# A new table of order, engines and buffer slots for a hand-scheduled attention and maxout kernel

## The chip, the cores and the metric

The kernel runs on one core of one Trainium2 chip. The metric is the time of one execution on the device in microseconds (us). The kernel before took 281.86 us, the median of three runs (281.57 to 282.61).

## What is computed

There are two stages. The first is linear attention with a feature map over exponentials; the second is a feed-forward layer that takes the largest of three products. The sizes are 8 batches, 8 heads, 576 positions, head size 64, 128 features; then 4,608 tokens of 512, a hidden size of 768.

```python
def phi(x):
    proj = np.einsum('bhsd,df->bhsf', x, w_phi)
    proj = proj - np.max(np.abs(proj), axis=-1, keepdims=True)
    return np.concatenate([np.exp(proj), np.exp(-proj)], axis=-1)
q_p, k_p = (phi(q), phi(k))
kv = np.einsum('bhsf,bhsd->bhfd', k_p, v)
z = np.sum(k_p, axis=2)
num = np.einsum('bhsf,bhfd->bhsd', q_p, kv)
den = np.einsum('bhsf,bhf->bhs', q_p, z)[..., None] + 1e-06
x = num / den                      # to [4608, 512]
h = np.maximum(np.maximum(x @ w1, x @ w2), x @ w3)
out = h @ w_out
```

## The kernel before

**Units and chunks.** The attention is cut into 16 units, each of four heads of one batch. Units 2b and 2b+1 together give the 512 features of batch b. The feed-forward layer is cut into nine chunks: chunk b takes the first 512 positions of batch b, and chunk 8 takes the last 64 positions of all batches.

**What one unit does.** POOL's queue loads q and k as bf16 (Lq, line 383, and Lk, line 393), SP's queue the last 64 positions of q (Lt, line 426) and v (Lv, line 435). For the first four units PE transposes q and k (T, line 459); for the others SP issues transposing DMAs (T, line 478). PE multiplies with the feature matrix (G, line 496, and M, lines 593 and 600). DVE takes the largest absolute values (rk and rq, line 500), ACT the exponentials of k (ek, line 504) and q (eq, line 584). POOL scales v by the exponentials of the maxima (va, line 548). PE multiplies keys by values (K, line 567) and queries by the result (N, line 632). DVE combines the two halves (xu, line 641; xw, line 644, which needs xu) and takes the reciprocal (xr, line 689). POOL divides (x, line 690). The result x is transposed into place by PE for the first two units (X, line 707), by SP's DMA for the others (X, line 722).

**What one chunk does.** PE multiplies x by differences of the weights (up and up2, line 748); ACT or DVE takes the positive part (t1), DVE the maximum (h). Then PE adds two products in one bank (straight, line 781; down, line 786), ACT or DVE copies the bank to a buffer `osb` (line 796), and SP's or ACT's queue stores it (line 800). There are four `osb` buffers: a copy may overwrite one only when its last store has landed.

**Row modes.** G, M (but its last one) and K use 64 of PE's 128 rows; all other matmuls use 128.

**What sets the order.** Nothing is scheduled by the framework. Every step is a node with its allowed engines, its dependences and its buffers. 1,565 nodes are listed in the order in which the program is made. The string `PLAN` (from line 88) has one word for each node, such as `753S2@135.0`: node 753, on SP (T is PE, D DVE, A ACT, G POOL, S SP), its buffers in the slots 2, and a start time by the planner's account. The words' order is the order of issue: each engine and each DMA queue runs its own nodes in that order, one behind the other. The start times are used once: `fill` puts idle matmuls on a tile of ones (line 911) into PE's gaps up to 30 us, so that PE is kept busy.

```python
for word in PLAN.split():
    what, start = word.split("@")
    at = next(i for i, c in enumerate(what) if c.isalpha())
    n, slots = nodes[int(what[:at])], iter(what[at + 1:])
    n.eng, n.start = ENGINES[what[at]], float(start)
    n.end = n.start + n.costs[n.eng] + 0.2
    for b in n.bufs:
        if b.index is None:
            b.index = int(next(slots), 36)
    order.append(n)
```

Nodes that the text names: 103 loads k of unit 1; 753 and 1031 load v of units 10 and 14; 749 loads q of unit 10 and 755 transposes it; 1267 and 1299 are stores, 1310 and 1302 copies into `osb`; 767 is an exponential of unit 10; 609 is the transposing DMA of x of unit 7; 666 is an N of unit 8; 1060 and 956 are steps of POOL for units 14 (va) and 12 (x); 1117 is a G of unit 15; 27, 106 and 110 are transposes by PE of units 0 and 1; 1553 is a down of chunk 8.

Of the kernel before, what the change touches and what calls it, by code (L numbers as in the profile page):

```python
# [88 lines left out]
9G0@1.2 10S0@0.8 3A@1.1 1D@0.8 2G@1.9 16S0@1.3 0G@2.1 103G1@2.7 104G@7.2 4A@1.8 12D@4.0 8G@7.5 6D@4.2 11A@4.0  # L89
19T0@4.5 5A@4.3 7A@4.6 20D0@5.2 25T1@5.8 187S1@2.9 13S@4.5 26D@6.4 29T23@6.3 102G@8.2 30A0@6.7 51T45@6.9 73T67@7.1 110T0@8.0  # L90
105S1@5.1 34A0@7.2 106T1@8.1 18S2@5.7 53D0@7.3 33A@7.7 32D0@7.9 35D@8.5 107D1@9.1 119T53@9.9 75A0@8.2 31A@8.7 260G2@8.9 77A@9.1
74A0@9.6 186G3@9.6 259G@10.4 111D@9.7 76A@10.1 112T21@10.1 188G@11.1 124A1@10.6 123A1@11.1 126T06@10.3 52D@9.9 128A@11.5 17G@11.3 122D1@10.5
115D@11.1 127A@11.8 1166G@11.5 15D@11.7 27T4@12.1 14D@12.0 117A@12.1 120A@12.5 121A@13.0 1167G@12.3 1169G@13.0 130D1@12.2 28D@12.5 43T76@12.8
21T4@13.0 261G@13.8 129D@12.7 46D@13.1 47D@13.5 54A0@13.6 113A@13.8 78T0@13.3 22D@13.8 36T56@14.3 118D@14.1 125D@14.7 56G0@14.0 44A@14.3
114A@14.5 79A@15.0 23T4@14.6 39D@15.3 40A@15.3 24D@15.9 42D@16.3 48T23@16.4 55G@15.1 137A1@15.8 139G1@16.2 80A@16.0 45A@16.2 50D@16.9
116A@16.5 185G@17.3 58A@17.0 108T4@16.7 37A@17.2 334S0@11.6 140G@18.0 263T0@17.2 57A@17.7 59G@18.2 60G@19.3 267T7@17.7 68T13@17.9 61G@20.4
38A@17.8 49D@17.5 81A0@18.3 109D@18.1 264D2@18.7 268D@19.3 41A@18.5 72A@18.9 71A@19.4 138G@20.5 141A@19.9 131T25@18.8 142G@21.6 144A@20.1
62T46@19.1 64A0@20.2 69A@20.3 63A@20.8 70A@21.0 134T07@19.7 132D@19.5 190T3@20.1 65T26@20.6 1168G@22.7 133D@20.1 156T54@21.2 135D@20.7 82T01@21.6
67A@21.4 66A@21.6 161T6@21.9 136D@21.3 158A1@21.7 191D3@21.8 85T27@22.1 159A1@22.2 143G@23.4 83D0@22.4 160A@22.7 86D@22.9 333G0@24.5 157A@23.2
84D@23.3 164A1@23.7 265T3@22.6 163A@23.9 87D@23.7 332G@25.2 162A@24.1 145T04@23.4 146A1@24.4 151T21@23.9 147A@24.5 194T5@24.3 266D@24.1 155A@24.7  # L100
152A@25.2 195D@24.7 1180T7@24.4 93T60@24.8 153A@25.6 88D0@24.9 89G0@26.0 1181D0@25.0 1172G@27.6 90T34@25.1 154A@26.1 94D1@25.6 148T57@25.7 149A@26.6
91D@26.0 283T62@26.3 1178T3@26.5 165T15@27.0 285A0@26.7 284A0@27.0 95D@26.4 92D@26.8 1176T0@27.3 150A@27.3 287D0@27.2 96D1@27.5 1179A@27.4 168T47@27.7
97G@29.7 286D0@27.6 335G@30.9 196T26@28.1 98T3@28.5 166D2@28.0 1177A@28.3 169D@28.4 200A1@29.2 198A1@29.7 176T14@28.9 197A@30.1 167D@28.8 170D@29.2
276T50@29.4 177D0@29.6 99D@30.0 277A@30.6 173T71@30.1 178D@30.4 100T3@31.0 171D2@30.8 202D1@30.9 1170G@31.1 174D@31.5 278A@31.1 281A@31.6 199D@31.9
280A@32.1 175D@32.5 172G1@33.2 1186T4@31.4 1184T7@32.7 192T2@34.0 279D@32.9 210T15@34.6 179D0@33.5 403G1@34.4 337S0@38.0 189S3@39.4 101A@32.5 1187A@33.1
180G@35.1 201A@33.6 203T34@34.7 1185A@34.2 282D@33.6 208A@35.1 1171G@36.3 1173G@38.4 205A@35.6 262S0@40.0 214D1@34.9 269T60@34.9 270A@36.1 274A@36.5
181T7@35.2 1182T5@35.5 1183A@37.0 193D@35.2 183T2@36.8 473S1@40.6 182D@35.8 209D@36.2 204A@37.5 1188T7@37.1 272D@36.8 184D@37.4 213D@37.8 206D@38.1
271A@38.0 1189A@38.6 1194T5@38.4 207A@39.0 301T26@39.3 212A@39.5 275D@38.7 1175G@40.5 294A0@39.8 402G@42.6 1174G@43.3 221A1@40.0 224A0@40.2 305A0@40.3
288T37@39.6 304A0@40.8 303A@41.2 211A@41.7 1195D1@39.4 338S@42.2 336S2@43.9 297A1@42.0 1202T4@39.9 273A@42.1 302A@42.6 404G@45.4 289D@40.0 223G@45.7
612S0@45.8 290D@40.6 1200T5@40.7 1196T3@41.6 222G@47.7 1203D@41.2 291T76@42.6 228T41@42.8 229A1@43.2 1201D@41.8 1197D@42.7 230A1@43.7 218T50@43.0 293D@43.3  # L110
1206T2@43.3 238T3@44.2 1192T6@44.3 220D@43.9 232A@44.2 219D@44.5 406S1@47.4 1207D@45.1 239A@44.6 240A@44.9 1193A@45.4 215T40@45.3 306T53@45.5 292D@45.7
231A@45.8 216D@46.2 217D@46.8 1214T2@45.8 1204T6@46.7 1215D@47.4 310A@46.3 1205D@48.0 307A@46.8 309A@47.3 475S1@50.0 1198T7@47.5 241A0@47.7 339T14@48.5
345D0@48.9 353T03@48.7 233T26@48.8 308A@47.9 1199A@48.6 357D1@49.5 237A@49.2 356D@49.8 342D@50.2 295G@49.8 296G@51.9 234A@49.7 1212T5@49.1 225T73@50.1
405S3@50.6 235A@50.2 236A@50.7 344A1@51.5 472G2@53.9 1213D@50.8 226D0@51.5 355A@51.9 346T26@51.3 227A@52.2 349D@51.8 352D@52.4 1210T5@51.7 1211D@53.0
340A1@52.5 471G@54.6 1208T7@52.5 343A@52.9 1209D@53.6 474G@55.4 242T34@53.6 542G3@55.6 354A@53.4 243D1@54.2 543G@56.3 341A@53.7 351A@54.1 245T50@53.9
246D@54.6 348A@54.6 244D@55.0 347A@55.1 350A@55.6 247D@55.4 298T71@54.3 300A1@56.1 253T35@55.6 250T42@55.9 364A1@56.3 367A0@56.5 314A1@56.6 299D@55.8
# [826 lines left out]
```

## Time and profile before

| What | before |
|---|---|
| median of the runs (lowest, highest) | 281.86 us (281.57, 282.61) |
| span of the profiled execution, first to last instruction | 280.8 us |
| PE, DVE, ACT, POOL busy, share of the span | 96%, 77%, 71%, 58% |
| granted clock of PE | 1.000 |
| packets of DMA, data moved | 76,214; 44.52 MB |

The profile gives the span of one execution; the runs' times also hold what lies around it. Busy time is the time in which an engine works; idle time is listed with what ended it. PE is the matmul unit, PEld its weight loads, DVE, ACT and POOL the vector, scalar and general units, SP the engine that only issues transfers; a name with q at its end is the engine's sequencer. The DMA share is the sum of the packets' times over that of the core's 16 DMA engines; packets overlap, so it can go over 1.

### The profile page before, as it was taken

To read this page: it belongs to the slowest core of one execution; us is meant where nothing else is said; L and a number is where in the kernel's file an instruction comes from. 1 tells how busy PE (TensorE), PEld (TensorE's weight loads), DVE (VectorE), ACT (ScalarE), POOL (GpSimd) and SP (SyncE) were. 2 spreads that over 40 slices of the span, in tenths; PEclk is the share of its full clock that TensorE was granted. 3 is DMA by queue.
4 is the path that set the end of the run, shared out by engine and by line. 5 is a ranking of instruction groups with operands and counts; after the bars stand their busy time and mean duration, and the time that the engine had idled before them with its cause. 6 is when DMAs were issued, how large, how long until landed. Compare 5 with 4: busy or idle time off the path is not lost. (4 is left out here: it accounts for less than half of the span.)

```text
span 280.8 us, 8401 instructions
## 1 busy us (share of the span) xinstructions
PE 268.3 (96%) x3409; PEld 150.8 (54%) x3447; DVE 217.3 (77%) x442; ACT 199.1 (71%) x489; POOL 161.5 (58%) x161
## 2 busy tenths in 40 slices
PE   8789899999999999999999999999999999999993
PEld 5457654576655555555555456655546544444441
DVE  2799989999999969889997899898876871157320
ACT  4799999999999787698978879989589200310001
POOL 4879999998949703897336848393495341000000
PEclk9999999999999999999999999999999999999999
DMA  7999999997999999999999997717130224110253
GB/s 136 300 202 208 207 173 310 260 164 132 171 186 249 236 196 281 169 171 144 189 263 204 188 276 125 151 55 170 39 86 3 77 47 121 40 75 0 82 144 112
DMA packets 76214, 44.52 MB, mean 159 GB/s; under 512 B 52688, under 2 KB 67344, under 8 KB 76176
## 3 DMA queue, kind: packets, MB, share of 16 engines
q1 hardware_dynamic: 59536, 29.21, 49.8%
q0 software_dynamic: 14912, 11.77, 28.7%
q10 hardware_dynamic: 1728, 3.02, 3.0%
q8 instruction: 27, 0.44, 0.7%
q14 instruction: 11, 0.09, 0.1%
HBM read 34.64 MB, written 9.44 MB: 157 GB/s over the span
## 5 line engine op out<-in xcount | busy, mean ns | idle before, releaser
L748 PE MATMUL ups<-xT,w_bf 128*128 128x512 bf16 x414 | 101.3, 379 | 1.0
L584 ACT ACTIVATE Eq<-psm 128x512 bf16<-128x512 f32 (+1 forms) x160 | 81.7, 587 | 5.4 <-PE psm L593 3.1
L548 POOL TENSOR_TENSOR vab<-v_raw,em 128x1152 bf16<-128x1152 f32 (+1 forms) x36 | 68.2, 1907 | 22.9 <-ACT em L542 15.0
L504 ACT ACTIVATE Ek<-psk 128x512 bf16<-128x512 f32 x128 | 72.1, 633 | 8.2 <-PE psk L496 6.3
L748 PEld LDWEIGHTS <-w_bf 128*128 128x128 bf16 x432 | 39.2, 98 | 43.9 <-issue 2.3
L690 POOL TENSOR_TENSOR x_sb<-y,rden 128x640 bf16<-128x640 f32 x32 | 39.9, 1256 | 39.5 <-DVE rden L689 39.0
L786 PE MATMUL ops<-wout_bf,hT 128*128 128x512 bf16 (+2 forms) x214 | 50.5, 373 | 0.3
L758 DVE TENSOR_TENSOR hT<-hT,ups 128x512 bf16<-128x512 bf16 x54 | 35.5, 677 | 13.3 <-PE ups L748 11.1
L500 DVE TENSOR_REDUCE mq<-psq 128x4 f32<-128x512 f32 x64 | 41.2, 682 | 3.5 <-PE psq L496 3.2
L500 DVE TENSOR_REDUCE mk<-psk 128x4 f32<-128x512 f32 x64 | 41.9, 679 | 2.1 <-PE psk L496 1.7
L762 ACT ACTIVATE hT<-ups 128x512 bf16<-128x512 f32 x36 | 21.9, 620 | 24.5 <-PE ups L748 24.4
L641 DVE TENSOR_TENSOR y<-psn,sq 128x325 f32<-128x325 f32 x64 | 30.4, 491 | 6.7 <-PE psn L632 4.3
L796 ACT COPY osb<-ops 128x512 f32<-128x512 f32 x20 | 12.2, 608 | 32.3 <-PE ops L786 31.8
L786 PEld LDWEIGHTS <-hT 128*128 128x128 bf16 x222 | 20.6, 98 | 22.5 <-issue 0.2
L632 PEld LDWEIGHTS <-Eq 128*128 128x128 bf16 x640 | 26.3, 98 | 10.3 <-issue 0.4
L644 DVE TENSOR_TENSOR y<-y,psn 128x325 f32<-128x325 f32 x64 | 29.7, 487 | 1.6
L632 PE MATMUL psn<-kv_sb,Eq 128*128 128x65 bf16 x640 | 28.8, 194 | 0.2
L496 PEld LDWEIGHTS <-qkT 64*128 64x128 bf16 x576 | 18.0, 94 | 13.4 <-issue 8.3
L781 PE MATMUL ops<-xT 128*128 128x512 bf16 x87 | 23.7, 380 | 0.5
L567 PE MATMUL kvps<-vab,Ek 64*128 64x65 bf16 x1152 | 22.1, 191 | 0.8 <-POOL vab L548 0.6
L567 PEld LDWEIGHTS <-Ek 64*128 64x128 bf16 x1152 | 20.3, 94 | 3.4 <-issue 1.3
L796 DVE COPY osb<-ops 128x512 f32<-128x512 f32 (+2 forms) x17 | 11.1, 657 | 12.5 <-PE ops L786 12.5
(65 smaller groups left out, 263.9 us busy)
## 6 DMA issues: line engine op xcount, KB each, us to landing
v_raw<-in_v_dram SPq DMA_DIRECT2D x15, 576.0 KB, 6.0
out_dram<-osb SPq DMA_DIRECT2D x23, 256.0 KB, 3.3
qk_bf<-in_k_dram POOLq DMA_DIRECT2D x15, 288.0 KB, 6.9
qk_bf<-in_q_dram POOLq DMA_DIRECT2D x15, 256.0 KB, 8.7
w_bf<-in_moe_w_dram POOLq DMA_DIRECT2D x3, 768.0 KB, 13.2
out_dram<-osb ACTq DMA_DIRECT2D x9, 256.0 KB, 3.4
tail_raw<-in_q_dram SPq DMA_DIRECT2D x16, 64.0 KB, 4.8
wout_bf<-in_moe_w_out_dram POOLq DMA_DIRECT2D x1, 768.0 KB, 19.2
```

The costliest lines, as they stand in the source:

```text
L500: return nd(kind, {"DVE": 0.598 if n == 4 else 0.331}, lambda: nc.vector.tensor_reduce(dst(m()), ps()[:, 0:n, :], AXX, ALU.max, apply_abso ...
L504: return nd("ek", {"ACT": 0.478 if n == 4 else 0.264}, lambda: nc.scalar.activation(dst(Ek[g]()), ps()[:, 0:n, :], EXP, scale=1.0 - 2.0 * ...
L548: made.append(chosen(n_, lambda n_, g=g, t0=t0, t1=t1: (nc.vector if n_.eng == "DVE" else nc.gpsimd).tensor_tensor(vab()[:, g, t0:t1, 0:D] ...
L567: nc.tensor.matmul(kvps[ab]()[:, pr, g, :], lhsT=Ek[g]()[r, t, :], rhs=vab()[r, g, t, :], start=(pr == prs[0] and g + j == 0), stop=(pr == ...
L584: return nd("eq", {"ACT": 0.478 if n == 4 else 0.264}, lambda: nc.scalar.activation(Eq[g]()[:, t0:t0 + n, :], ps()[:, 0:n, :], EXP, scale= ...
L632: nc.tensor.matmul(psn[g]()[:, i, :], lhsT=Eq[g]()[:, t, :], rhs=kv()[:, pr, ab, g, :], start=True, stop=True)
L641: n_ = nd("xu", {"DVE": 0.064 + 0.0676 * n_t}, lambda: nc.vector.tensor_tensor(yv(y()), ps(0), sq_of(sq()).unsqueeze(len(shape) - 1).to_br ...
L644: return nd("xw", {"DVE": 0.064 + 0.0674 * n_t}, lambda: nc.vector.tensor_tensor(yv(y()), yv(y()), ps(1), ALU.add), [n_], [psn[1], y], loc ...
L690: divs[pr] = nd("x", {"POOL": 1.2}, lambda pr=pr, y=y, rden=rden: nc.gpsimd.tensor_tensor(x_sb()[:, pr].rearrange("p t a d -> p a t d"), y ...
L748: nc.tensor.matmul(ups()[:, o * n:(o + 1) * n], lhsT=w_bf[i + (not plain)][:, ct, jj * P:(jj + 1) * P], rhs=tokens_of(ct)[:, cols] if halv ...
L758: nc.vector.tensor_tensor(dst, dst, src, ALU.max)
L786: nc.tensor.matmul(ops_()[:, 0:hi - lo], lhsT=hT()[:, j, tt * P:(tt + 1) * P], rhs=wout_bf[:, j, lo:hi], start=plain and j == 0, stop=(j = ...
```

## The change

Only the string `PLAN` is replaced. The nodes, their work, their sizes and the number of buffers stay. The new table was laid out with an account of when the last part of each transfer lands and of a gap at each change of row mode. It holds the same 1,565 nodes in another order, on other engines where there is a choice, and in other slots. The counts by table:

| What | before | after |
|---|---|---|
| changes of row mode in PE's order | 98 | 94 |
| loads of v issued by SP, by ACT | 15, 1 | 11, 5 |
| copies into `osb` by ACT, by DVE | 20, 17 | 27, 10 |
| positive parts (t1) by ACT, by DVE | 36, 18 | 32, 22 |
| copies of K's result (kv) by ACT, by DVE | 26, 10 | 22, 14 |

A cut of the diff: the first lines, and those that hold the nodes named above.

```diff
-9G0@1.2 10S0@0.8 3A@1.1 1D@0.8 2G@1.9 16S0@1.3 0G@2.1 103G1@2.7 104G@7.2 4A@1.8 12D@4.0 8G@7.5 6D@4.2 11A@4.0
...
-625A1@102.3 529D@102.3 819G@94.0 537D@102.7 633A1@102.8 1294T0@103.0 632A@103.0 530D0@103.1 1285D@103.3 628A@103.3 749G@94.7 629A@103.8 1280T4@103.9 538D1@103.9
...
-753S2@135.0 1324T1@136.4 758A@137.8 781A1@138.3 1303A@138.5 736D@136.8 1325D@137.5 757A@139.0 740T34@137.3 741D2@138.1 1326T5@137.6 743T21@138.5 737D@138.5 738D1@139.1
...
-1031A1@155.0 1033S3@150.2 963S@151.5 1366T5@154.4 1030G@155.0 806D1@154.6 851G@155.2 1356T4@155.3 1367D@155.5 868A0@155.6 1357A@156.4 917T13@156.3 909T67@156.5 913D1@156.8
...
+3A@0.7 1D@0.8 4A@1.3 10S0@0.7 9G0@1.2 103G1@1.9 0G@2.6 16S0@1.1 104G@4.9 17G@5.1 11D@3.5 7D@3.7 5D@3.9 8G@5.3 6D@4.1 12A@3.5 19T0@4.0
...
+616S@95.3 1029S1@96.4 574G@100.1 1283A@103.9 633A@104.3 700T35@103.8 526D@103.4 530D0@103.8 1259S@97.6 635D1@104.0 753A0@104.6
...
+594D@115.4 749G@112.6 755S@117.6 595D@115.8 599D2@116.2 662A0@117.0 698A@117.2 646T07@116.1 659T5@117.3 695A@117.7 660A@118.2
...
+768A1@121.2 661A@121.7 1309T@121.3 663T75@122.6 710D@121.6 1267S@118.7 712G1@120.2 1300T2@122.9 769D1@122.2 664D2@123.2 722A0@122.0
+721A0@122.4 1310A3@122.9 767A1@123.4 1030G@122.3 766D@123.5 671T71@123.8 666T36@124.1 667D@124.6 668D@125.0 672D1@125.4 609S@119.1
+1299A@123.9 890S0@120.5 720A@124.5 764A@124.9 1515G@123.5 1514G@124.3 1301T@124.4 824S@121.7 674T36@125.7 765A@125.4 719A@125.9
+728T7@126.0 1302A1@126.7 714G@125.1 1027G@125.3 1032S1@122.8 1322T4@126.1 1323A0@127.2 730A@127.7 675D@126.2 673D@126.7 676D@127.0
...
+1409D@184.4 1395D@185.2 1048T52@185.1 1045A@184.9 1049A@185.4 1050A@185.7 1031A2@185.9 1052D1@185.8 1051D@186.2 993T16@185.2
```

More of the change, by code (lines that the diff above doesn't have):

```diff
@@ L93 @@
[L93 to L104, printed above, removed]
@@ new lines @@
+1084D@211.1 1418D3@211.5 1419S@212.3 1431S@212.7 1088T53@211.4 1146A@211.9 1439A1@212.1 1450T7@211.7 1152T26@212.6 1089D1@212.1
+1085D@212.5 1086D2@212.9 1153D2@213.1 1090D@213.5 1451D@213.9 1154D@214.5 1442T1@212.9 1432T5@213.7 1433A@214.8 1087G2@213.2
+1149T02@214.6 1150D@215.1 1151D@215.5 1436T3@214.9 1091T76@215.8 1440T5@216.1 1452T0@216.9 1443A@215.3 1092D@216.3 1093D@216.7
+1094D1@217.1 1095G@217.4 1096S@218.8 1446T2@217.8 1155D0@217.2 1437A@216.0 1144A@216.5 1157T17@218.7 1158D0@219.2 1159D@219.6
@@ new lines @@
+1487D@236.8 1493D@237.6 1470A3@232.9 1472T5@237.4 1478T1@238.3 1476T4@239.1 1477A@240.2 1479D@239.4 1491D@240.0 1467A@240.7
+1494T0@240.0 1495D@241.1 1522T3@240.9 1484T4@241.7 1473D@241.7 1485D@242.8 1526T1@242.6 1496T7@243.5 1508T0@244.3 1488T5@245.2
+1542T4@246.1 1462A1@241.3 1527A@243.7 1524T2@246.9 1463S@241.9 1523D@243.4 1489D@246.3 1534T1@247.8 1535D@248.8 1458D0@249.4
+1532T3@248.6 1509T@249.5 1510A2@251.0 1511A@251.5 1530T5@250.8 1540T1@251.7 1525D@250.1 1541D@252.7 1536T6@252.5 1531D@253.3
@@ L202 @@
+"""
 ENGINES = {"T": "PE", "D": "DVE", "A": "ACT", "G": "POOL", "S": "SP"}
```

217 lines of the change are left out of this document (121 added, 96 removed).

## The prediction

> **What bounds the kernel now.** I read the page first, then busy time by stretches, then what PE waited for.
>
> ```profile
> span 280.8 us, 8401 instructions
> ...
> PE 268.3 (96%) x3409; PEld 150.8 (54%) x3447; DVE 217.3 (77%) x442; ACT 199.1 (71%) x489; POOL 161.5 (58%) x161
> ```
>
> ```profile
> core 0: us, PE busy (x) PEld busy (x) DVE busy (x) ACT busy (x) POOL busy (x), PEclk, DMA share, GB/s
> 0.00:33.00 33.00, 28.72 (x478) 20.04 (x478) 25.58 (x59) 26.93 (x74) 26.63 (x40) 1.00 1.12 211
> 33.00:75.00 42.00, 40.73 (x605) 23.86 (x614) 39.57 (x83) 41.18 (x104) 40.78 (x34) 1.00 1.06 202
> 75.00:150.00 75.00, 74.31 (x1004) 41.09 (x1018) 67.63 (x140) 64.48 (x155) 45.69 (x43) 1.00 1.22 208
> 150.00:155.00 5.00, 4.31 (x121) 2.92 (x117) 3.60 (x6) 4.00 (x9) 2.84 (x3) 1.00 1.20 179
> 155.00:277.00 122.00, 120.23 (x1212) 62.89 (x1228) 80.90 (x158) 62.51 (x152) 45.52 (x44) 1.00 0.41 99
> 277.00:281.00 4.00, 0.00 (x0) 0.00 (x0) 0.00 (x0) 0.00 (x0) 0.00 (x0) 1.00 0.40 115
> ```
>
> PE is the bound, and the clock is full throughout, so only PE's idle time can be won: 280.8 - 268.3 = 12.5 us. Some 4 of them lie behind its last matmul, 4.3 in the first 33 us. From 33 to 75 us DVE, ACT and POOL are as full as PE (39.57, 41.18, 40.78 of 42): there PE could not run ahead of them anyway. From 75 to 155 us PE alone is full, and the packets' times fill the 16 DMA engines 1.22 times over. After 155 us everything but PE has room.
>
> The longest waits of PE's own work, and the place of the last one:
>
> ```profile
> PE tps L459 <- DMA qk_bf<-in_k_dram: 1.6, 1, 1.6
> ...
> PE pxT L707 <- issue: 0.7, 1, 0.7
> PE kvps L567 <- POOL vab L548: 0.6, 1, 0.6
> ```
>
> ```profile
> 148.49 2.12 POOL L548 TENSOR_TENSOR vab<-v_raw,em 128x1152 bf16<-128x1152 f32 x1 [1.55 <-DMA v_raw<-in_v_dram]
> ...
> 152.89 1.04 PE L567 MATMUL kvps<-vab,Ek 64*128 64x65 bf16 x54 [0.64 <-POOL vab L548]
> ```
>
> POOL stood 1.55 us for a v load, and PE paid 0.64 of it.
>
> How far may the times in the table be used? Only as distances, and only because the trace follows them:
>
> ```profile
> 9.34 0.72 PE L459 MATMUL tps<-ident,qk_bf 128*128 128x128 bf16 x10 [1.60 <-DMA qk_bf<-in_k_dram]
> ...
> 273.26 2.47 PEld L786 LDWEIGHTS <-hT 128*128 128x128 bf16 x12
> ```
>
> These are entries 110 and 106 (written for 8.0 and 8.1) and entry 1553 (written for 268.7): late by 1.3 and by 4.6. So 260.7 us of the table took 263.9 on the chip, 1.2% more. A distance of 5 us in the table is 5 us on the chip, if nothing between waits. The question is whether transfers fit the distances that the new table leaves.
>
> **The change part by part.** Matmuls, copies and transfers are the same in number; their work is costed at nothing. What changes is who waits.
>
> *Start.* The first transpose waits for the first half of k in both tables: no gain. The 1.60 us wait is for k of unit 1 (entry 103), which now goes ahead of the identity and of a memset:
>
> ```profile
> 2.13 0.22 POOL L330 MEMSET wph_low<- 64x128 bf16 x1
> ...
> 2.81 0.73 POOL L393 DMA_DIRECT2D qk_bf<-in_k_dram  x1
> ```
>
> It is issued 0.68 us sooner, so at best 0.7 of the wait goes. All of the table's lead is bound from above by its two ends, 271.3 against 269.3: 2.0 us. But the time passes through the stretch where DVE is as full as PE, and the new order puts more dependent pairs there:
>
> ```profile
> 24.78 0.49 DVE L641 TENSOR_TENSOR y<-psn,sq 128x325 f32<-128x325 f32 x1
> 25.18 0.89 DVE L644 TENSOR_TENSOR y<-y,psn 128x325 f32<-128x325 f32 x2
> ```
>
> Two independent ones take 0.89, the second starting 0.40 after the first; one that needs the other's result waits its whole 0.49, 0.09 more. Counting DVE instructions that directly follow the one they need, up to 80 us, I find 2 in the old table and 22 in the new one: 20 x 0.09 = 1.8 us of DVE. Bounds -2.0 and +1.8; I take +0.5, since 0.7 of gain against 1.8 of loss is +1.1, and DVE is not full in the first 33 us (25.58).
>
> *Row mode.* Both tables leave about 0.1 us at a change between 64-row and 128-row matmuls; the changes go from 98 to 94. What one costs:
>
> ```profile
> 51.86 1.04 PE L748 MATMUL ups<-xT,w_bf 128*128 128x512 bf16 x4
> 52.83 0.24 PE L567 MATMUL kvps<-vab,Ek 64*128 64x65 bf16 x4
> ```
>
> ```profile
> 252.03 7.77 PE ups L748 x36
> ```
>
> At 7.77 / 36 = 0.216 each, four matmuls issued from 51.86 end at 52.72; the other mode starts at 52.83: 0.11. Four fewer: -0.4.
>
> *The v load of unit 10.* It was entry 753 on SP, 8.5 us ahead of its use; now on ACT, 31.4 ahead. The 0.64 us go; late next for K is only POOL's product itself, 2.12 us long, for which the table leaves its full time: -0.6.
>
> *A new tight chain at 112 to 128 us.* POOL issues q of unit 10 (749@112.6). SP's transpose 755@117.6 waits for it; behind it on SP stand store 1267@118.7, the x transpose 609 and a tail load. The store must land before ACT's copy 1310@122.9 may overwrite its buffer; behind that copy on ACT stands 767, whose bank PE's 666@124.1 needs. Next, store 1299@123.9 must land before ACT's copy 1302@126.7. Distances: 5.0 for the load, 4.2 and 2.8 for the stores. The old table leaves never under 6.2 between a store and the reuse of its buffer. Measured: q loads from 30 to 160 us, stores from 80 to 155, v loads of the whole run:
>
> ```profile
> L383 POOL DMA_DIRECT2D qk_bf<-in_q_dram x11: 750/760/811, 44.4 to 158.6; - x11
> ...
> DMA to landing us min/median/max: 4.9/8.3/12.0
> ```
>
> ```profile
> L800 SPq DMA_DIRECT2D out_dram<-osb x10: 343/534/1148, 81.8 to 154.9; - x10
> ...
> L800 ACTq DMA_DIRECT2D out_dram<-osb x3: 338/354/372, 86.5 to 142.6; - x3
> ...
> DMA to landing us min/median/max: 3.3/6.1/8.5
> ```
>
> ```profile
> L435 SPq DMA_DIRECT2D v_raw<-in_v_dram x15: 368/575/1439, 4.6 to 190.1; - x15
> ...
> L435 ACTq DMA_DIRECT2D v_raw<-in_v_dram x1: 458/458/458, 158.8 to 158.8; - x1
> ...
> DMA to landing us min/median/max: 4.4/6.2/9.4
> ```
>
> At the shortest landings only the last store is late, 3.3 - 2.8 = +0.5. At the medians it is 3.3 + 1.9 + 3.3 = +8.5. The medians come partly from loads issued four in a row, and this one goes alone; so I take 6.5 for the load (+1.5), 5.0 for the first store (+0.8) and 3.3 for the second (+0.5): +2.8.
>
> *The v load of unit 14.* Entry 1031, on ACT, 3.6 us ahead of its use 1060 on POOL; late by 0.8 at the shortest landing, by 2.6 at the median. Behind 1060 stands the division 956, which frees a buffer for DVE, which frees a bank for PE's 1117; about 1.4 us of the table's distances lie between. So 0 to +1.2; I take +0.4, as few transfers run there (share 0.41). The Trainium skill ("DMA: Bandwidth & Descriptors", "Anatomy of one DMA") puts a transfer at about 2.0 us plus bytes over 436 GB/s, an estimate of 3.4 us for these 576 KB, and by it this term would be 0. The trace disagrees: none of 16 landed under 4.4.
>
> *SP to ACT.* Five v loads instead of one go by ACT, 0.46 us of ACT's queue each against 0.58 of SP's. The one that did so landed after 9.4, the longest of all:
>
> ```profile
> v_raw<-in_v_dram ACTq DMA_DIRECT2D x1, 576.0 KB, 9.4
> ```
>
> The same page of the Trainium skill ("Issuing engines are not separate DMA queues") says that this saves issue time alone, as the 16 DMA engines are shared; by that rule, too, the landings above stay as they are. I add nothing.
>
> *End.* Both tables end with a copy and a store on ACT; the 4 us stay.
>
> Sum: 0.5 - 0.4 - 0.6 + 2.8 + 0.4 = +2.7, a span of 283.5. The median of the runs, 281.86, lies 1.1 us over the span; with these the forecast is **284.6 us**.
>
> **The rivals.** *The early lead holds and the transfers fit (faster).* The place is the first 33 us: if DVE's dependent pairs fall where it has room, the lead of the table counts, -1.4 (0.7 of the k load, and as much again from the second half of unit 0, whose transposes, entry 27, stand at 10.1 instead of 12.1); with -0.4, -0.6 and only +0.5 at unit 10: -1.9, 280.0 us. It decides when q of unit 10 lands within 5 us and the stores within 3.3. For it: the shortest q landing is 4.9. Against: the DMA share of 1.22 just there.
>
> *The transfers fit, but no early lead (same).* 0.5 - 0.4 - 0.6 + 0.5 + 0 = 0: 281.9 us. By the Trainium skill's figure above it would come out so.
>
> *Everything lands at the medians (much slower).* 0.5 - 0.4 - 0.6 + 8.5 + 1.2 = +9.2: 291.1 us. For it: in the new table the 30 us from 105 hold eight qkT transposes where the old one holds four.
>
> *The row-mode gap does nothing.* Both tables have it, so the words of the change promise more than 0.4 us can hold; this is in all sums.
>
> **How the numbers follow.** Forecast 0.40, much slower 0.11, same 0.27, faster 0.22. Slower by over 0.5% (1.4 us, about what a measurement of this kernel can tell from no change) is 0.51, within 0.27, faster 0.22. The range leaves out half of the two outer cases: 280.2 to 289.5. As both signs hold much, the likeliest case alone runs from 283.3, where slower begins, to 287.0, where the chain at unit 10 costs 5.2.
>
> **What would show it.** Right: ACT's copies into osb idle for out_dram transfers near 123 to 130 us, and PE then waits on ACT or on POOL; no PE wait for vab near 150; PE's wait for k near 8 us shorter; DVE over 95% full up to 75 us. Wrong: PE idle under 0.5 us from 105 to 135 (then unit 10's chain fits); the PE position after 40 us more than 1 us ahead of the old one (then the early lead is real); or q of unit 10 landing within 5 us.

## The result and the profile after

After: 307.64 us, the median of four runs (303.09 to 312.81), against 282.01 for the kernel before on the same chip (281.57 to 282.61). The ratio is 1.0789 [1.0736, 1.0841]: slower by 22 us, where 2.7 were forecast, and far outside the range. The profiled execution is a run of 310.01 us, and two of the four, it among them, were longer than the other two: where the runs of a kernel fall apart so, the ratio, here and below, rests on the shorter ones.

The page of the kernel after; line numbers are now higher by 26.

```profile
span 308.2 us, 8412 instructions
...
PE 278.4 (90%) x3435; PEld 152.8 (50%) x3435; DVE 220.1 (71%) x444; ACT 201.4 (65%) x488; POOL 161.1 (52%) x160
...
PEclk9999995799999995999999999999999999999998
DMA  7999999208999999599899992697205123011234
```

PE has 29.8 us idle, the DMA line has a hole, and the clock falls twice. Each slice is 7.7 us: the first fall lies from 46 to 62 us, the hole (2 and 0) from 54 to 69, the second fall from 116 on. The windows of the kernel after, first those shown of before, then the two places:

```profile
core 0: us, PE busy (x) PEld busy (x) DVE busy (x) ACT busy (x) POOL busy (x), PEclk, DMA share, GB/s
0.00:33.00 33.00, 28.28 (x456) 19.30 (x456) 25.18 (x59) 27.22 (x68) 26.94 (x44) 1.00 1.09 206
33.00:75.00 42.00, 31.94 (x399) 16.95 (x396) 29.27 (x56) 28.29 (x72) 28.75 (x19) 0.88 0.76 149
75.00:150.00 75.00, 68.40 (x964) 37.75 (x963) 60.64 (x126) 58.30 (x142) 44.99 (x41) 0.95 1.12 180
...
155.00:277.00 122.00, 119.83 (x1446) 64.13 (x1444) 93.61 (x187) 79.55 (x194) 58.57 (x54) 1.00 0.57 118
...
45.00:50.00 5.00, 0.00 (x0) 0.00 (x0) 0.00 (x0) 0.60 (x2) 1.61 (x1) 0.69 1.13 254
50.00:55.00 5.00, 3.88 (x17) 1.43 (x17) 3.59 (x6) 4.88 (x12) 0.41 (x1) 0.50 0.96 308
55.00:60.00 5.00, 5.00 (x33) 2.10 (x32) 3.31 (x6) 3.22 (x7) 5.00 (x3) 0.79 0.18 66
60.00:65.00 5.00, 5.00 (x42) 2.25 (x41) 4.94 (x10) 4.88 (x17) 1.49 (x2) 1.00 0.01 3
...
115.00:120.00 5.00, 1.22 (x4) 0.55 (x4) 0.00 (x0) 0.00 (x0) 0.00 (x0) 0.52 1.33 188
```

The first 33 us and the stretch after 155 us are as full as before. Nearly all is lost between: 8.8 us of PE's work are missing from 33 to 75 us (31.94 against 40.73), and in 45 to 50 us no engine but ACT and POOL does anything. What PE waited for in the kernel after:

```profile
PE ups L774 <- ACT xT L744: 9.6, 1, 9.6
PE ups L774 <- DMA xT<-x_sb: 5.9, 2, 3.8
```

Neither has a row in the profile before. The timeline of the kernel after around the first (start, duration, in brackets the idle time before and what ended it):

```profile
37.74 0.62 ACT L895 CAST xT<-pm 128x512 bf16<-128x512 f32 x1
...
48.93 0.42 ACTq L461 DMA_DIRECT2D v_raw<-in_v_dram  x1
49.40 1.08 ACT L530 ACTIVATE Ek<-psk 128x512 bf16<-128x512 f32 x2 [11.04 <-DMA qkT<-qk_bf]
50.37 0.70 ACT L744 COPY xT<-pxT 128x640 bf16<-128x640 bf16 x1
...
51.12 1.87 PE L774 MATMUL ups<-xT,w_bf 128*128 128x512 bf16 x4 [9.60 <-ACT xT L744]
...
54.59 2.12 POOL L574 TENSOR_TENSOR vab<-v_raw,em 128x1152 bf16<-128x1152 f32 x1 [7.98 <-ACT em L568]
```

ACT ends a copy at 38.36 and does nothing until its queue issues a v load at 48.93: that is entry 189, the v load of unit 2, `189S3@39.4` in the old table and `189A0@33.6` in the new one. Behind it stand the exponentials, the copy of x that PE needs, and POOL's vab. The row names its releaser, a transposing DMA of q and k; the one under way is entry 406, for unit 5. It is found by its line and issue time:

```profile
L504 SPq DMA_TRANSPOSE qkT<-qk_bf x1: 1469/1469/1469, 43.6 to 43.6; - x1
...
  ACT Ek L530: 11.0, 1
...
DMA to landing us min/median/max: 5.4/5.4/5.4
```

Issued at 43.6, landed 5.4 later at 48.9; the v load went out at 48.93. Yet a load of v for unit 2 needs nothing from a transpose for unit 5.

**Where 27.4 us (308.2 less 280.8) went.** I compared when PE had issued the same share of all its matmul columns in the two profiled executions: +0.8 us at 8% of the columns, +13.2 at 14%, +14.6 at 30%, +22.1 at 35%, +22.0 at 40%, +25.1 at 50%, +26.5 at the last matmul, and +0.9 behind it. Some matmul records are missing from the traces, so each figure is good to about half a microsecond. So 12.4 at the first stop, 7.5 at the second, 3.1 where the prediction's chain lies, and 4.4 in the rest.

### The profile page after: what moved, and what is told of

Read it like the earlier page. It is cut to its first block, busy times and chain, and to the rows that moved or that the text cites. A ratio compares the mean times of both kernels' runs of the same rounds, so it can differ in the third digit from the quotient of the medians.

```text
span 308.2 us, 8412 instructions
## 1 busy us (share of the span) xinstructions
PE 278.4 (90%) x3435; PEld 152.8 (50%) x3435; DVE 220.1 (71%) x444; ACT 201.4 (65%) x488; POOL 161.1 (52%) x160
## 3 DMA queue, kind: packets, MB, share of 16 engines
q1 hardware_dynamic: 58304, 26.58, 43.6%
## 4 chain that ended last, share of the span: by engine, by line
PE 49%; DMA 5%; POOL 4%; issue 3%; DVE 2%; ACT 0%; POOLq 0%; DVEq 0%; ACTq 0%
PE ups L774 21%; PE ops L812 11%; PE ops L807 7%; DMA xT<-x_sb 5%; PE psn L658 3%; PE kvps L593 3%; POOL vab L574 3%; PE psq L522 1%; PE psk L522 1%; PE psm L619 1%; POOL x_sb L716 1%; DVE y L670 0%; DVE y L667 0%; PE pst L522 0%; DVE mk L526 0%
## 5 line engine op out<-in xcount | busy, mean ns | idle before, releaser
L774 PE MATMUL ups<-xT,w_bf 128*128 128x512 bf16 x432 | 105.9, 389 | 16.0 <-ACT xT L744 9.6
L774 PEld LDWEIGHTS <-w_bf 128*128 128x128 bf16 x432 | 40.3, 99 | 62.7 <-issue 22.1
L716 POOL TENSOR_TENSOR x_sb<-y,rden 128x640 bf16<-128x640 f32 x32 | 39.9, 1255 | 30.3 <-DVE rden L715 30.1
L812 PE MATMUL ops<-wout_bf,hT 128*128 128x512 bf16 (+2 forms) x222 | 51.7, 373 | 0.0
L526 DVE TENSOR_REDUCE mk<-psk 128x4 f32<-128x512 f32 x64 | 42.2, 682 | 12.1 <-ACT Ek L530 10.9
L788 ACT ACTIVATE hT<-ups 128x512 bf16<-128x512 f32 x32 | 19.2, 607 | 30.2 <-PE ups L774 30.0
L822 ACT COPY osb<-ops 128x512 f32<-128x512 f32 (+1 forms) x27 | 16.1, 595 | 29.7 <-PE ops L812 28.4
L670 DVE TENSOR_TENSOR y<-y,psn 128x325 f32<-128x325 f32 x64 | 31.0, 490 | 4.8 <-PE psn L658 0.5
L658 PEld LDWEIGHTS <-Eq 128*128 128x128 bf16 x640 | 27.0, 97 | 12.4 <-issue 2.6
L812 PEld LDWEIGHTS <-hT 128*128 128x128 bf16 x222 | 20.5, 98 | 22.1 <-issue 0.5
L658 PE MATMUL psn<-kv_sb,Eq 128*128 128x65 bf16 x640 | 29.8, 194 | 1.7 <-DVE y L667 0.7
L522 PEld LDWEIGHTS <-qkT 64*128 64x128 bf16 x576 | 18.8, 95 | 16.2 <-issue 11.8
L807 PE MATMUL ops<-xT 128*128 128x512 bf16 x96 | 24.8, 382 | 0.1
L593 PE MATMUL kvps<-vab,Ek 64*128 64x65 bf16 x1152 | 22.1, 191 | 2.0 <-issue 1.2
L790 DVE TENSOR_SCALAR hT<-ups 128x512 bf16<-128x512 f32 x22 | 14.9, 682 | 11.7 <-PE ups L774 11.7
```

What stands on the lines that cost most here:

```text
L526: return nd(kind, {"DVE": 0.598 if n == 4 else 0.331}, lambda: nc.vector.tensor_reduce(dst(m()), ps()[:, 0:n, :], AXX, ALU.max, apply_abso ...
L593: nc.tensor.matmul(kvps[ab]()[:, pr, g, :], lhsT=Ek[g]()[r, t, :], rhs=vab()[r, g, t, :], start=(pr == prs[0] and g + j == 0), stop=(pr == ...
L658: nc.tensor.matmul(psn[g]()[:, i, :], lhsT=Eq[g]()[:, t, :], rhs=kv()[:, pr, ab, g, :], start=True, stop=True)
L716: divs[pr] = nd("x", {"POOL": 1.2}, lambda pr=pr, y=y, rden=rden: nc.gpsimd.tensor_tensor(x_sb()[:, pr].rearrange("p t a d -> p a t d"), y ...
L774: nc.tensor.matmul(ups()[:, o * n:(o + 1) * n], lhsT=w_bf[i + (not plain)][:, ct, jj * P:(jj + 1) * P], rhs=tokens_of(ct)[:, cols] if halv ...
L807: nc.tensor.matmul(ops_()[:, 0:hi - lo], lhsT=tile_of(ct, tt), rhs=line_w[c_i > MOVE][:, ct, lo:hi], start=(ct == 0), stop=False)
```

## The theories

**First stop: the rotation.** In the built program each transfer on SP's and ACT's queues signals one of eight completion semaphores. They are given in rotation over both queues together, in the order in which the program lists the transfers, and a transfer waits until the one eight places ahead, the last user of its semaphore, has landed. Entry 189 is listed behind SP's transfers up to one written for 49.7, so eight ahead of it is 406, which is written for 44.0, 10 us after 189 itself. ACT issues in order, so its whole queue waits. The rival: issuing a v load from ACT costs this anywhere, or ACT's transfers wait for any transpose in flight.

**Second stop: the x transpose of unit 5.** Entry 470 is written 4.9 us ahead of chunk 2's first up in the new table (87.8 and 92.7), 9.4 in the old one (88.1 and 97.5). If its landing takes over 4.9, PE waits. The rival: it is only the first stop that bunches transfers there.

A note on the edits: the text ahead of the prediction says that the words' order is the order of issue and that the start times serve only the idle matmuls. That is not so. `fill` returns the steps sorted by their start times, so a start time changed in the table moves its step on its queue. That is all that most edits do. The order in which the built program lists the transfers, by which the rotation counts, does not follow the start times everywhere, as entry 189 shows; what sets it was not followed up.

## Experiments

**v2_act_28, v2_act_30, v2_sp: entry 189 elsewhere.** Three kernels from the new table, the v load of unit 2 on ACT earlier by two amounts, or back on SP:

```diff
-189A0@33.6
+189A0@28.0   (v2_act_28)
+189A0@30.3   (v2_act_30)
+189S0@41.2   (v2_sp)
```

> The new table with one word changed: the v load of unit 2 (entry 189) stays on ACT's queue, written for 28.0 instead of 33.6. Theory: in the changed kernel ACT stood at this load from 38.4 to 48.93 us because it waits for the completion semaphore that the transfer eight places ahead of it in SP's and ACT's common rotation holds, and that is the transposing DMA of unit 5 (entry 406), which landed at 48.91. At 28.0 the transfer eight places ahead is a tail load (entry 334) that landed at 14.88: no wait, ACT passes in 0.4 us, the 10.5 us and the 2 us of slow clock behind them go. If the starved transfers near 110 to 120 us come from the hole that this stop leaves in the DMA engines at 55 to 70 us, their 7 us go too: 284 to 287 us. If they are the new table's own: 291 to 294. Rival 1 (a v load on ACT's queue is held by the load's own transfer or its queue, whatever stands ahead of it): it still stands some 10 us, 303 to 306. Rival 2 (ACT's load waits for transposing DMAs in flight): none is in flight before 39.8, so no stop either; the run with 30.3 tells that one apart.

> The new table with the v load of unit 2 on ACT's queue, written for 30.3. The transfer eight places ahead is then the v load of unit 3 on SP (entry 262), which in the changed kernel was issued at 42.67 and landed at 47.60. Theory: ACT reaches the load near 34.8 us and stands until that landing, 12 to 13 us, a little more than the 10.5 of the changed kernel: 303 to 308 us, and ACT goes on within 0.1 us of the landing. Rival 2 (it waits for transposing DMAs in flight): none is in flight at 34.8, no stop, and the time is that of the kernel at 28.0.

> The new table with the v load of unit 2 put back on SP's queue, between the two transposing DMAs of unit 4 (41.2). Theory: as with 28.0 on ACT, no stop on ACT, 284 to 287 us if the later starved stretch goes with it, 291 to 294 if not; the load lands near 46 and POOL's product of unit 2 waits for it by at most 1 us. Rival 1 (a v load on ACT's queue is slow in itself): the same here, so this run and the one at 28.0 would differ by 10 us or more. Rival 3 (SP is what runs late, with one more transfer on it): 0.6 us slower than the one at 28.0 for its issue.

Measured, with 282.57 for the kernel before beside them: v2_act_28 289.57 in the profiled execution, 296.55 to 302.42 in three others, which have no profile (no ratio is drawn from so wide a spread); v2_act_30 306.07 and 305.61, ratio 1.0811 [1.0738, 1.0884]; v2_sp 297.74, ratio 1.0475 [1.0367, 1.0583].

At 28.0, eight ahead is an early tail load; the timeline of v2_act_28 shows no stop:

```profile
31.78 0.42 ACTq L461 DMA_DIRECT2D v_raw<-in_v_dram  x1
```

At 30.3, eight ahead is the v load of unit 3 (entry 262, issued at 43.0, landed at 47.7). The timeline of v2_act_30:

```profile
47.74 0.42 ACTq L461 DMA_DIRECT2D v_raw<-in_v_dram  x1
48.21 2.55 ACT L530 ACTIVATE Ek<-psk 128x512 bf16<-128x512 f32 x5 [10.63 <-DMA v_raw<-in_v_dram]
```

The stop stays, and its releaser changes from a transpose to a v load, as the rotation says and "any transpose" does not. Whatever stands eight places ahead holds ACT. In all the kernels of this list that stop, the landing and the issue agree within 0.1 us:

```
kernel           transfer on ACT     eight places ahead     landed     issued
after            189, v of unit 2    406, T of unit 5        48.91      48.93
v2_act_30        189                 262, v of unit 3        47.7       47.74
v2_act_28        189                 a tail load             long ago   31.78, no stop
clear_x5         614, a v load       544, v of unit 7       109.82     109.89
before           1227, a store       1219, a store           86.45      86.52
before_x5_late   1227                751, a tail load        88.34      88.41
```

In the kernel after, the store 1307 went out on ACT at 140.47 while a transpose was in flight (137.94 to 143.19), so transposes as such hold nothing up.

v2_sp has no first stop and still pays the second. By the runs the first stop costs 1.0789 - 1.0475 = 0.031, about 9 us; in the profiled execution of after it was 12.4.

The second stop, in v2_act_28 and v2_sp, by the row of entry 470 in each. In v2_act_28:

```profile
L748 SPq DMA_TRANSPOSE xT<-x_sb x1: 1329/1329/1329, 95.3 to 95.3; - x1
...
DMA to landing us min/median/max: 3.8/3.8/3.8
```

In v2_sp:

```profile
L748 SPq DMA_TRANSPOSE xT<-x_sb x1: 3623/3623/3623, 95.2 to 95.2; - x1
...
DMA to landing us min/median/max: 10.9/10.9/10.9
```

The same transfer, issued at the same time to 0.1 us, lands after 3.8 or after 10.9; by the position of PE, v2_sp is 2.5 us behind the kernel before at 30% of the columns and 9.8 at 35%, while v2_act_28 stays at 2.4. So the second stop needs no first one, and the rival falls.

Entry 470 is not the whole of it. In v2_sp PE waits twice, first for the x transpose of unit 4 (entry 401):

```profile
102.70 0.63 PE L774 MATMUL ups<-xT,w_bf 128*128 128x512 bf16 x2 [2.54 <-DMA xT<-x_sb]
...
106.16 1.01 PE L774 MATMUL ups<-xT,w_bf 128*128 128x512 bf16 x2 [2.83 <-DMA xT<-x_sb]
```

Entry 401 is written 11.4 us ahead of the up (81.3 and 92.7; 12.5 in the old table). It landed 8.1 after its issue in v2_act_28, 13.3 in v2_sp and 12.5 in after, where it makes 2.1 of the 5.9 us in the row of waits above. So room for 470 alone would not have covered the stop, and why transposes land so late there stays open.

The windows from 95 us on, v2_act_28 and then v2_sp:

```profile
95.00:100.00 5.00, 5.00 (x105) 2.96 (x105) 4.32 (x9) 5.00 (x13) 3.10 (x3) 1.00 1.23 228
```

```profile
95.00:100.00 5.00, 5.00 (x107) 2.99 (x104) 4.33 (x9) 4.53 (x12) 3.03 (x3) 1.00 1.40 88
100.00:105.00 5.00, 0.80 (x8) 0.22 (x3) 1.22 (x3) 1.77 (x4) 0.00 (x0) 0.81 1.35 158
```

The DMA engines are as full in one as in the other (1.40 and 1.23), but move 88 GB/s against 228. A share over 1 does not tell which of the two a stretch will be.

**before_v2_act: the same move in the old table.** The v load of unit 2 goes to ACT, where eight places ahead has long landed.

```diff
-189S3@39.4
+189A3@38.5
```

> The kernel before with the v load of unit 2 moved from SP's to ACT's queue, written for 38.5. The transfer eight places ahead is a tail load (entry 334) that landed at 17.77. Theory: ACT passes it in 0.4 us; ACT is full in that stretch, so 0 to +0.6 us: 281.6 to 282.6. Rival 1 (a load on ACT's queue is slow in itself): ACT stands for 5 us or more, 287 or over.

Measured: ten runs from 280.84 to 289.51, median 287.13; ratio 0.9953 [0.9897, 1.0010], which rests on 280.84 and 281.69 alone; the eight others took 285.71 or more. In the profiled run, one of the eight, the load went out at 39.52 with no stop on ACT. So a v load on ACT does not by itself stop ACT, and the rival to the rotation falls. What the move costs in time stays open: in that profile transfers jam from 157 us on, the transposing DMA of unit 13 lands after 14.6 us (3.2 in before), the v load of unit 12 after 15.9 (8.7 in before), and POOL waits 8.4 us for it. So the old table can jam too; what starts it was not found.

**before_x5_late: the second stop put into the old table.** Entry 470 is moved to 4.3 us ahead of the up that needs it.

```diff
-470S@88.1
+470S@93.2
```

> The kernel before with one transfer moved: the transposing DMA of x of unit 5 (470) goes behind a v load (614), a transpose (684), a store (1263) and another transpose (754), from 88.1 to 93.2, 4.3 us instead of 9.4 ahead of chunk 2's first up. Theory: 470 is issued near 99.5 and lands 4 to 11 us later, while PE wants it at 100.6: 3 to 9 us slower, 285 to 291 us, and scattered. Rival: the distance doesn't matter since PE has other work: 281.5 to 283.

Measured: 290.9 (289.19 to 292.91) against 281.76, ratio 1.0340 [1.0278, 1.0402]. PE's waits in before_x5_late:

```profile
PE ups L748 <- DMA xT<-x_sb: 4.2, 1, 4.2
PE psk L496 <- ACT Eq L584: 1.9, 1, 1.9
```

One word moved by 5 us on SP costs 0.034 x 281.76 = 9.6 us. The transfer landed 7.7 after its issue, and PE stood 4.2. The second row was not meant: it is the rotation again. Moving one SP transfer shifted which transfer stands eight ahead of ACT's store 1227; a timeline row of before_x5_late, where before has 86.52:

```profile
88.41 0.36 ACTq L800 DMA_DIRECT2D out_dram<-osb  x1
```

So the price is not of the distance alone; 4.2 of the 9.6 is its direct part.

**clear_x5, clear2: room for entry 470 in the new table.** Both start from v2_act_28 and move loads and transposes that have room out of the way of entry 470.

```diff
 (clear_x5)
-685S3@70.8  683S3@73.1  820G@83.6  1028G1@78.0
+685S3@93.5  683S3@107.0 820G@93.1  1028G1@95.5
 (clear2; 685 stays)
-683S3@73.1  820G@83.6  1028G1@78.0
+683S3@107.0 820G@101.9 1028G1@107.0
```

> As v2_act_28 (the v load of unit 2 on ACT at 28.0), and four transfers that are used 30 to 50 us later are moved from ahead of the transposing DMA of x of unit 5 (entry 470) to behind it: on SP the transpose of q of unit 9 (685, from 70.8 to 93.5) and the v load of unit 9 (683, from 73.1 to 107.0), on POOL's queue the k loads of units 11 (820, from 83.6 to 93.1) and 14 (1028, from 78.0 to 95.5). Theory: the second stop of the changed kernel is chunk 2's first up (entry 1272), which the table starts 4.9 us after entry 470; 470 landed 3.8 us after its issue in the profile of v2_act_28 (289.57 us) and 10.9 in that of v2_sp (297.12). With less queued ahead it lands within 5 us in every execution: 287 to 290 us, all runs within 2 us of each other. Rival: the landing varies by itself, whatever is queued; then the runs stay spread from 289 to 302.

> As v2_act_28, and three loads that are used 20 to 50 us later are moved behind the transposing DMA of x of unit 5, this time further on and without the transpose 685, which in clear_x5 stood 7.8 us at its own issue with three loads in flight and held all of SP's queue: on SP the v load of unit 9 (683, to 107.0), on POOL the k loads of units 11 (820, to 101.9) and 14 (1028, to 107.0). Theory: what is in flight ahead of entry 470 decides the second stop; 470 lands within 5 us and nothing new is bunched: 286 to 290 us, runs within 3 us of each other. Rival: the 16 DMA engines are full from 75 to 135 us in the new order whatever is moved by a few places, and the stop comes back elsewhere: 294 to 300.

Measured: clear_x5 298.09, ratio 1.0575 [1.0531, 1.0619]; clear2 296.21, ratio 1.0499 [1.0461, 1.0538]. In both, 470 lands after 3.5, and PE's long wait for it is gone. The time is not: the stop moves. In clear_x5 the transposes behind it jam, and entry 614 on ACT is held by the rotation until the v load of unit 7 has landed; later PE waits for a transpose directly:

```profile
100.72 11.42 SPq L504 DMA_TRANSPOSE qkT<-qk_bf  x3
109.89 0.40 ACTq L461 DMA_DIRECT2D v_raw<-in_v_dram  x1
...
138.48 0.61 PE L522 MATMUL psk<-wph,qkT 64*128 64x128 bf16 x8 [5.39 <-DMA qkT<-qk_bf]
```

The second is the longer of the two: by its position PE loses about 2 us at the stop of entry 614, and 7 to 9 around 135. In clear2 the transposes jam near 120, and PE waits for them in the same way:

```profile
120.27 16.27 SPq L504 DMA_TRANSPOSE qkT<-qk_bf  x3
...
136.62 0.61 PE L522 MATMUL psk<-wph,qkT 64*128 64x128 bf16 x8 [5.90 <-DMA qkT<-qk_bf]
```

Three transposes take SP 16.27 us to issue, where the shortest single ones took 1.3 each. Moving three or four words gave the jam a new place. That the new table keeps transposes and POOL's loads too close to each other is a reading of these rows; no run shows it alone.

Part of what both lose lies in their first 30 us, ahead of all that was moved; it is read under "The start" below.

**clear_x5_warm, clear_x5_chain, clear2_q10, clear2_q10_warm: the prediction's own terms on top.** "Warm" puts more idle matmuls into PE's first microseconds, "chain" and "q10" give the chain of unit 10 room: stores and the x transpose ahead of it, or the q load 6.4 us earlier.

```diff
 (warm, both kernels)
-19T0@4.0  29T12@5.0  25T3@5.3
+19T0@4.45 29T12@5.25 25T3@5.75
 (clear_x5_chain, without warm)
-755S@117.6 1267S@118.7 609S@119.1
+755S@118.3 1267S@117.2 609S@117.8
 (clear2_q10)
-749G@112.6
+749G@106.2
```

> As clear_x5, and the first three PE entries (19, 29, 25) are written for 4.45, 5.25 and 5.75 instead of 4.0, 5.0 and 5.3, in the same order, so that more idle matmuls are put ahead of them. In before, PE's idle matmuls of 256 columns took 0.215 us until 4.7 us and 0.11 from 4.9, after 3.8 us without a pause; in the changed kernel PE pauses from 3.38 to 4.05 and they take 0.215 until 10.2. Theory: without the pause the faster pace comes near 5 us, the transposes of unit 1 (entry 110) start near 9.4 to 9.8 us instead of 10.5, and the whole is 0.8 to 1.5 us faster than clear_x5. Rival (the recorded one: DVE's dependent pairs make the start late): DVE sets the time up to 75 us, no more than 0.3 us faster.

> As clear_x5, and on SP's queue near 117 us the store 1267 and the transposing DMA of x of unit 7 (609) go ahead of the transposing DMA of q of unit 10 (755): 117.2, 117.8, 118.3 instead of 118.7, 119.1, 117.6. Theory, the prediction's chain of unit 10: in v2_act_28 755 waited for its q load until 126.2, store 1267 behind it landed at 131.66, ACT's copy 1310 began at 131.73 (0.7 us late), and 609, behind both, landed at 133.0, for which POOL's copy 1515 stood until 133.18 (1.7 us late); PE lost 2.5 us there against the kernel before. Out of 755's way they land 3 us sooner: 1.8 to 2.7 us faster than clear_x5. Rival: POOL and DVE are late there by themselves, and the order on SP is worth less than 0.5 us.

> As clear2, and the q load of unit 10 (749) goes 6.4 us earlier on POOL's queue, from 112.6 to 106.2, right behind the k load 750. Theory, the prediction's chain of unit 10: the transpose 755 no longer waits for its load, the store 1267 and the transposing DMA of x of unit 7 (609) behind it on SP go out on time, ACT's copy 1310 and POOL's copy 1515 start without a wait: 1.5 to 2.5 us faster than clear2. Rival: no more than 0.5 us.

> As clear2_q10, with the first three PE entries later (4.45, 5.25, 5.75), so that idle matmuls fill PE's pause at 3.4 us. In clear_x5_warm the transposes of unit 1 (entry 110) then started at 8.96 us instead of 9.5 to 10.5. Theory: what PE is ahead at 30 us stays: 0.8 to 1.5 us faster than clear2_q10. Rival: DVE, ACT and POOL are full from 33 to 75 us and take it back: within 0.4 us of it.

Measured ratios to before: clear_x5_warm 1.0568 [1.0525, 1.0612] and clear_x5_chain 1.0555 [1.0521, 1.0590], beside 1.0575 for clear_x5; clear2_q10 1.0499 [1.0455, 1.0543] and clear2_q10_warm 1.0454 [1.0407, 1.0501], beside 1.0499 for clear2. Every interval overlaps that of its base: no term shows. For the chain that decides nothing, since in these kernels the jam covers it (the q load issued 6.4 us earlier still had its transpose wait behind the two that jam).

**before_v10, before_k1, before_cold, before_k1_v10: the small terms in the old table.** In their profiles nothing jams, and 12 runs each resolve about half a microsecond.

```diff
 (before_v10)  -753S2@135.0 +753S2@131.0
 (before_k1)   -103G1@2.7   +103G1@1.85
 (before_cold) -19T0@4.5    +19T0@4.1
```

> The kernel before with one transfer moved: the v load of unit 10 (753) goes ahead of the transpose 893 on SP, from 135.0 to 131.0. In the profile of before it was issued at 140.25, landed at 148.33, and POOL and then PE waited for it (PE 0.64 us). No transfer of ACT's queue gets another place in the rotation. The prediction's term: -0.6 us, 281.0 to 281.5 where before has 281.5 to 282. Rival: 893 and what follows on SP are 0.6 us later and take it back: within 0.2 us.

> The kernel before with the k load of unit 1 (103) ahead of the two memsets on POOL's queue, from 2.7 to 1.85, as in the new table. It is issued 0.7 us sooner; PE waited 1.6 us for it near 8 us. The prediction's bound: -0.7 at best; by its belief that DVE, ACT and POOL, full from 33 to 75 us, take it back, 0. Rival: the identity, made 0.7 us later, holds the first transposes: +0.3 or more.

> The kernel before with PE's first entry (19) written for 4.1 instead of 4.5: two idle matmuls fewer stand ahead of it, so that PE pauses from 3.6 to 4.3 us as it does in the new table. Theory: PE's matmuls go at the slow pace (0.215 us for 256 columns) to about 8 to 10 us instead of 4.7, and the start is 0.5 to 1.5 us later, in the whole time too. Rival: the pace near 5 us is back at once (within 1 us), or PE's place at 10 us isn't what binds: within 0.3 us of before.

> Both of the edits before_v10 and before_k1, the two parts of the new table that the prediction held to be gains: -0.6 to -1.3 us against before by its terms, 280.2 to 281.2; rival: within 0.3 us of before.

Measured against 282.34 (281.1 to 286.56):

| Kernel | median | ratio | |
|---|---|---|---|
| before_v10 | 281.71 | 0.9988 [0.9965, 1.0012] | wait for vab gone from the profile |
| before_k1 | 281.68 | 0.9981 [0.9963, 0.9999] | T of unit 1 starts at 8.36 instead of 9.34 |
| before_cold | 282.30 | 1.0007 [0.9988, 1.0027] | two idle matmuls fewer: no change seen |
| before_k1_v10 | 281.91 | 0.9972 [0.9954, 0.9989] | both edits |

PE's transpose of unit 1 in before_k1, where before has `9.34` and a wait of 1.60 for the load:

```profile
8.36 0.72 PE L459 MATMUL tps<-ident,qk_bf 128*128 128x128 bf16 x10 [0.41 <-POOL qk_bf L430]
```

before_k1_v10 is faster than before by 0.8 us, though its own profile shows a wait for k of 1.2 again; what it owes to which edit is not settled. The wait varies without any edit: before_v10, whose first 130 us are those of before, starts this transpose at 8.98. So not all of the step from 9.34 to 8.36 is the edit's.

## Why the prediction was wrong, point by point

**The step that failed: "A distance of 5 us in the table is 5 us on the chip, if nothing between waits".** The condition was taken for granted, and the steps listed for it were only the named buffers' own. Shown: a transfer on ACT also waits for the transfer eight places ahead in both queues' common order, and where that one is written later, the table's order cannot hold.

**"SP to ACT. … I add nothing": mis-sized by 9 to 12 us.** Here the queue that a transfer is moved to was priced by its issue time, 0.46 us. The Trainium skill ("DMA: Bandwidth & Descriptors", "Issuing engines are not separate DMA queues") says that issuing from several engines saves only issue time; I read into it that the move could not cost more either. What the issue waits for, and what stands behind it on ACT, was the cost: 10.6 us from 38.36 to 48.93. Not all five moved v loads cost this: among ACT's transfers in the new table, 189 is the only one whose predecessor is written for a later time than its own.

**The list of tight distances left out a kind.** I searched loads, stores and their buffers and found unit 10. I never laid the transposing DMAs of x against the up that reads them: 4.9 us for unit 5 where the old table has 9.4. Landings between 3.5 and 11.4 were measured for this one transfer, so 4.9 is too short. The transpose of unit 4 went from 12.5 to 11.4 us ahead of the up, and it too came late. In before's trace the two transposes of x between 85 and 100 us landed after 3.5 and 4.9, so the view would have called 4.9 tight at once; how far such a landing can stretch is the new thing. Cost: 7.5 us in after.

**The chain of unit 10: place and size about right, the branch wrong.** v2_act_28 shows it without the first two stops:

```profile
120.45 0.81 POOL L409 DMA_DIRECT2D qk_bf<-in_q_dram  x1
...
128.41 0.52 SPq L826 DMA_DIRECT2D out_dram<-osb  x1
129.49 1.35 SPq L748 DMA_TRANSPOSE xT<-x_sb  x1
...
131.73 0.59 ACT L822 COPY osb<-ops 128x512 f32<-128x512 f32 x1 [0.63 <-DMA out_dram<-osb]
...
133.18 0.40 POOL L922 COPY xT<-xT 64x256 bf16<-64x256 bf16 x1 [2.56 <-DMA xT<-x_sb]
```

The q load landed at 126.20, after 5.75 (I took 6.5); the store after 3.25 (I took 5.0); ACT's copy into `osb` then waited for it, as forecast, but only 0.63. The longer branch was the one I listed and did not price: the x transpose of unit 7 behind the store, which holds POOL for 2.56. By its position PE lost 2.6 us there against before (+2.3 at 40% of the columns, +4.9 at 50%), where +2.8 stood in the sum. Only part of that can be seen as waits: PE's idle time from 115 to 146 us is 1.27 us, and from 105 to 135 it is 0.39, which the prediction had named as the sign that the chain fits. So the nearness of 2.6 to 2.8 is partly luck, and the branch is read from the rows, not tested alone.

**The start.** +0.5 was forecast; v2_act_28 stands +1.4 to +1.7 at 5 to 10% of the columns, after +0.8. The gain from the earlier k load shows as half a microsecond in before_k1, with an interval that reaches almost to none. What was overlooked is when PE gets its full pace. The same ten idle matmuls, in v2_act_28 and then in clear2, whose words up to 73 us are the same:

```profile
8.61 2.32 PE L937 MATMUL idler<-idle 128*128 128x256 bf16 x10
```

```profile
7.58 1.59 PE L937 MATMUL idler<-idle 128*128 128x256 bf16 x10
```

With the late pace the transposes of unit 1 start at 10.72 in v2_act_28 (10.11 in after), with the early one at 9.04 in clear2. But an early PE then stands for the q load of unit 2, and the clock falls to half. The transpose and the window in clear2:

```profile
18.22 1.03 PE L485 MATMUL tps<-ident,qk_bf 128*128 128x128 bf16 x8 [1.81 <-DMA qk_bf<-in_q_dram]
```

```profile
18.00:25.00 7.00, 6.66 (x112) 4.38 (x112) 4.23 (x9) 3.97 (x12) 5.61 (x9) 0.51 1.25 205
```

In the four kernels with the new table whose PE waits there for 1.07 us or less (after, v2_act_28, v2_sp, clear2_q10_warm) the clock is full from 18 to 25 us; in the six where it waits for 1.39 to 1.94 it falls. That the wait is the reason is not tested. Either way this table loses in its first 30 us: clear2, 1.7 us ahead of v2_act_28 at 1% of the columns, is 1.2 behind it at 5%, where v2_act_28 is itself 1.7 behind before. In the old table before_cold has two idle matmuls fewer and shows no change, but its full pace came back early, at 5.9 us, so it does not price a late one.

DVE was over 95% full to 75 us, as forecast: in v2_act_28 40.66 of 42 from 33 on. The price of its dependent pairs was too low. A row of two in after, the second of which needs the first's result:

```profile
71.08 0.49 DVE L667 TENSOR_TENSOR y<-psn,sq 128x325 f32<-128x325 f32 x1
71.67 0.49 DVE L670 TENSOR_TENSOR y<-y,psn 128x325 f32<-128x325 f32 x1
```

The second starts 0.59 after the first, where independent ones follow after 0.40: 0.19 more, not 0.09, and 20 of them come to 3.8 us of DVE. What that is worth in time was not tested alone.

**The v load of unit 10, -0.6.** Its wait vanished in before_v10 and the time with it by -0.12% [-0.35, +0.12]: 0.3 us, within the noise. In v2_act_28 PE waits for a vab again, 0.61 us at 138.31, this time of unit 9.

**Idle time as a bound.** "Only PE's idle time can be won" took the busy time for work that cannot stretch. v2_act_28 spans 7.0 us more than before, but its PE is idle for 13.3 us against 12.5; the other 6.2 us stand in the profile as busy time (274.5 against 268.3). One way is in the page's rows: a matmul of 512 columns is counted as busy for 0.379 us, while the next may start 0.216 after it, so short delays between matmuls stay hidden. Missing records work the other way (x3409 matmuls against x3447 weight loads in before), but 9.2 of before's 12.5 us lie in seven gaps of over 0.25 us, so they can fill only some of the other 3.3.

**The v load of unit 14, +0.4, and the end, 0.** That load landed 3.9 us after its issue in v2_act_28 and in after, sooner than the 4.4 taken as the least, and yet POOL stood for it:

```profile
200.85 2.12 POOL L574 TENSOR_TENSOR vab<-v_raw,em 128x1152 bf16<-128x1152 f32 x1 [5.29 <-DMA v_raw<-in_v_dram]
```

PE falls back by about 0.9 us in the stretch that follows; that the load is the reason was not tested. Behind the last matmul lie 5.6 us in both kernels, where before has 4.6: +1.0 for a term that was put at nothing.

**Unsettled.** In v2_act_28, 7.0 us over before in span, 4.4 lie outside the chain: 2.3 before it, 2.1 behind it, of which the two terms above are nearly all. Why three of its four runs were 7 to 13 us longer than the profiled one was not seen; that 470 landed late in them (as in v2_sp) or that the clock fell at 18 us (as in clear2) is argued from other kernels alone.

## What to carry to other kernels

When a transfer goes to another engine's queue, ask first what its issue waits for, and what stands behind it on that engine: a semaphore shared in rotation over two queues ties a load to a stranger that is written for later. Lay every transfer against its first reader, in the old order and the new one, and treat any distance that shrank to the usual landing time as a likely stop, above all in a stretch with the DMA engines full. In such a stretch here, moving a few transfers mended one place and spoiled another, so let the measured landings, not the wait that is shown, say whether the table has room.

## What the runs showed of the hardware

**The clock after a stop.** PE resumed at 51.12 after 9.6 us; its granted clock was 0.50 from 50 to 55 us, 0.79 from 55 to 60 and full from 60 on, so about 6 us at half speed. Four matmuls of 512 columns took 1.87 us there, 0.47 each against 0.216. The Trainium skill ("TensorE: Matmul & The Clock Gate", "What's actually happening") gives half clock after an idle window of about 3.4 us and full clock after one of sustained work; the halving agrees, and full clock came back about 6 us after the restart, which is under two such windows. So a long stop costs more than its length: PE's busy time is 278.4 in after, which has two such falls, and 274.5 in v2_act_28, which has none, for the same matmuls.

**A stopped queue empties the others.** While ACT stood, POOL waited behind it (7.98 us before vab), and after the restart the DMA share fell to 0.18 and 0.01: the transfers that should have run in the stop had run, those behind POOL had not been issued.

**The landing of a transposing DMA has a long tail.** Entry 470, the same bytes every time: 3.5, 3.8, 7.7, 10.9 and 11.4 us in clear_x5 and clear2, v2_act_28, before_x5_late, v2_sp and after.
